# A fused attention, MoE and mixer kernel: the first third of the channel weights is combined before the token layer, and chunk 0's channel inputs are made before batch 1's first token product

## The chip, the cores and the metric

The kernel runs on one core of a Trainium2 chip. The metric is the time of one execution in microseconds (us), lower is better. The kernel before took 513.13 us (median of three runs, 512.84 to 515.15).

Engines are named as the profile names them: PE (TensorE, matmuls), PEld (its weight loads), DVE (VectorE), ACT (ScalarE), POOL (GpSimd) and SP (SyncE, which here only issues DMAs). Each runs its own list of instructions in order; semaphores tie the lists together.

## The reference

Three layers follow each other, on 2 batches of 768 tokens and 512 features.

```python
x = attention(q, k, v)                    # 8 heads, window and block sums
x = sigmoid(xr @ w_r) * (relu(xk @ w_k)**2 @ w_v)        # "MoE" layer
h = relu(x.T @ w_tok1) @ w_tok2           # token mixing, 768 -> 256 -> 768, per batch
u = x + h.T
out = u + relu(u @ w_ch1) @ w_ch2         # channel mixing, 512 -> 1536 -> 512
```

The weights arrive as 64-bit numbers and all products are made to about float32 precision.

## The kernel before

**Numbers in pairs.** Every operand of a product is split into a rounded part "hi" and a rest "lo", and `mm3` (L525 to L532) makes each product of three matmuls: hi by hi, hi by lo, lo by hi. ACT makes hi with a cast, DVE or POOL makes lo with a subtraction (`rounded`, L171 to L174; on L806 for the token layer's inputs `y`). So no product starts before its lo parts are there.

**Weights.** `Weights.step` takes one 128 x 512 piece of a weight matrix. SP has loaded it as 64-bit words into the slot (`wst`) that it will fill; ACT scales the upper words (L152), DVE puts the two halves together (a shift on L156 and a shift-or on L162), and then the pair is made on ACT and POOL. Pieces wait in one list and are taken in turn, one `step` at a time, at places that the code sets by credits.

**The channel layer's first product** is made by a Strassen scheme: seven products (`part(1)` to `part(7)`) of sums of quarter blocks take the place of eight. Its weights are therefore combined, not just split. `Fold.close` takes two pieces and makes of them, on DVE, POOL and ACT, the pairs that the seven products use: two sums by DVE or POOL of 128 x 512 elements, one of 128 x 256 by POOL, and four rounded pairs whose lo parts POOL makes. Two folds (d = 0 and 1) make one third (g = 0, 1, 2) of `w_ch1`. The unpacked pieces lie in a tile `f4` (`f` in the profile).

**The channel layer's inputs** are combined likewise, once per chunk of 512 tokens, by `chan_prep`. PE transposes four token tiles into `utr` (L841), ACT copies them into two tiles `f4`, and `first`, `second` and `third` make the pairs `u` for the seven products. All sums are DVE's (the default of `sums`, L184); of the lo parts, d = 0 is POOL's and d = 1 is DVE's:

```python
eng = nc.gpsimd, nc.vector
sums(pr[d], eng[d], (0, f[:, 1], f[:, 3], ALU.subtract), (1, f[:, 2], f[:, 0], ALU.subtract), tag=tags[d])
```

**The order of the work.** The attention and the MoE layer's first two products run interleaved; the loop over `gates` (the sigmoid product `ro`, L691 to L705) ends the MoE layer. Then `c_phase` runs, for batch 0 and batch 1: `y_split` (pairs of the token layer's input), `tok1` (36 matmuls into `h1`, in the profile `h`), `tok2` (36 into `ho`; L826 adds them to `ybuf`, the running result of all tokens). Before `d_phase`, the channel layer, stands `chan_prep(0)`:

```python
        yield from tok2(0, h0)
        h1 = yield from tok1(yy)
        uu = {}
        yield from chan_prep(0, uu)
        yield from tok2(1, h1)
```

Chunk 0 holds tokens 0 to 511 of batch 0, so it needs `tok2(0)` and nothing of batch 1. The code's order is a priority; a scheduler then sets each engine's order when the kernel is built, so that neighbouring steps overlap. `tc.high_priority(n)` moves steps ahead by n.

**Slots.** `wa` and `wb` (8 each) held the MoE layer's weights, `R2` (12, of which 10 are used) those of the gates and the token layer. When the MoE layer's tiles are free, pool `w2` is laid over them. In the kernel before, the second channel weights `w_ch2` (`c2_add`) go to `wb` and are first in the list of weights; `c1_add(0)` and `c1_add(1)` come behind them, into a ring `CR` of `w2`'s slots and freed ones.

Of the kernel before, what the change touches and what calls it, by code (L numbers as in the profile page):

```python
# [10 lines left out]
F32R = mybir.dt.float32r  # L11
# [38 lines left out]
AHEAD3 = 2  # L50
WF = 2
HC = 256
OB = 2


@with_exitstack
def fused_kernel(ctx, tc, q, k, v, vt, mu, w_k, w_v, w_r, w_t1, w_t2, w_c1, w_c2, out):
    nc = tc.nc
# [8 lines left out]
    KD = DM // 128  # L67
# [6 lines left out]
    CH = 512  # L74
# [5 lines left out]
    def bank(tag, bufs, shape, name):  # L80
        return ps.tile(shape, F32, tag=tag, bufs=bufs, name=name)

    const = pool("const", "left")
    ident = const.tile([128, 128], F32, name="ident")
# [8 lines left out]
    ys = [ybuf[:, i] for i in range(B * NT)]  # L93
# [18 lines left out]
    class Ring:  # L112
# [3 lines left out]
        def next(self):  # L116
            self.i += 1
            return self.slots[(self.i - 1) % len(self.slots)]
# [117 lines left out]
    weights = Weights()  # L236
# [4 lines left out]
    wa, wb = Ring(r1, "wa", NRA), Ring(r1, "wb", NRB)  # L241
# [436 lines left out]
    R2 = Ring(r2, "w", 12)  # L678
# [33 lines left out]
    for got in hidden:  # L712
# [4 lines left out]
        if len(wr) == KD:  # L717
            credit += (got or 0.0) * GRATIO
            while credit > 0:
                g = next(gates, None)  # L720
# [7 lines left out]
    U = Ring(r1, "u", 0)  # L728
    U.slots = wa.slots[:7]
    spare = wa.slots[7:]  # L730

    def c1_add(g):
        for d in range(2):
            fold = Fold(c1[g], CR, d, LEND[g][d])
            for z in (d, d + 2):
                weights.add(CR, w_c1[z * 128:(z + 1) * 128, :].rearrange("p (h f) -> p h f", h=2)[:, :, HC * g:HC * g + HC], fold)

    def tiles(g):
        return [2 * g, 2 * g + 1], [NF2 // 2 + 2 * g, NF2 // 2 + 2 * g + 1]

    def c2_add(c, g):
        for f in sum(tiles(g)[::-1], []):
            weights.add(wb, w_c2[f * 128:(f + 1) * 128, :], lambda pr, f=f: c2_have(f, pr))

    kept = ctx.enter_context(tc.tile_pool(name="kept", bufs=1, space=bass.MemoryType.DRAM))
    stored = {}
# [1 line left out]
    def c2_have(f, pr):  # L748
        c2[0, f] = pr
        t = stored[f] = kept.tile([128, 2, 512], F32, tag=f"w{f}", bufs=1, name="stored")  # L750
        for i in range(2):
            nc.sync.dma_start(t[:, i], pr[i].bitcast(F32))

    def c2_back(c, g):
        for f in sum(tiles(g)[::-1], []):
            t = wb.next().tile([128, 2, 512], F32R, "w")
            nc.gpsimd.dma_start(t, stored[f])  # L757
            c2[c, f] = t[:, 0], t[:, 1]

    c2_add(0, 0)  # L760
    credit = 0.0
    for got in gates:
        credit += got or 0.0
# [5 lines left out]
    xp.release()  # L769
    work.release()  # L770
    w2 = pool("w2", "left", reuse_waits="tile")
    CR = Ring(w2, "w", 21 - 12 - len(spare))
    CR.slots = spare + CR.slots + R2.slots[R2.i % 12:] + R2.slots[:R2.i % 12]
    LEND = CR.slots[12:14], CR.slots[14:15] * 2, (None, None)
    c1_add(0)
    c1_add(1)
    c2_add(0, 1)

    def new_f4():
        return w2.tile([128, 4, HC], F32, tag="f4", bufs=2, name="f4")  # L780
# [19 lines left out]
    def y_split(b):  # L800
        yy = []
        for s in range(NT):
            hi, lo = U.next().split("y")
            y = ys[b * NT + s]
            nc.scalar.copy(hi, y)
            (nc.vector if s % 2 else nc.gpsimd).tensor_tensor(lo, y, hi.bitcast(F32), ALU.subtract)  # L806
            yy.append((hi, lo))
        return yy

    def tok1(yy):  # L810
        hh = []
        for m in range(NM):
            o = bank("acc", MT, [128, DM], "h1")
            yield from mm3(o, [(cut(t1[s], m * 128, 128), yy[s]) for s in range(NT)])
            hh.append(relu_split(o))
        return hh

    def tok2(b, hh):
        for s0 in range(0, NT, 2):
            os = [bank(*(("s", 2) if s0 % 4 == 0 else ("acc", MT)), [128, DM], "ho") for _ in range(2)]  # L820
            for m in range(NM):
                for j in range(2):
                    yield from mm3(os[j], [(t2[s0 + j][m], hh[m])], first=(m == 0), last=(m == NM - 1))
            for j in range(2):
                y = ys[b * NT + s0 + j]
                nc.vector.tensor_tensor(y, os[j], y, ALU.add)  # L826
# [7 lines left out]
    def chan_prep(c, u):  # L834
        if c:
            fold_all()
        f4 = [new_f4() for _ in range(2)]
        for z in range(KD):
            tp = bank("pt", 2, [128, CH], "utr")
            for t in range(NQ):  # L840
                nc.tensor.transpose(tp[:, t * 128:(t + 1) * 128], ys[c * NQ + t][:, z * 128:(z + 1) * 128], ident)  # L841
            n = z // 2 * 2
            nc.scalar.copy(f4[z % 2][:, n:n + 2].rearrange("p a n -> p (a n)"), tp)
            yield 0.43
        eng = nc.gpsimd, nc.vector
        tags = (None,) * 6 if c else ("m3", "m4", "o", "o", "mw", "m4")

        @ahead(HM)
        def first():
            pr = [pieces(U.next(), "u") for _ in range(3)]  # L850
            for d in range(2):
                f = f4[d]
                sums(pr[d], eng[d], (0, f[:, 1], f[:, 3], ALU.subtract), (1, f[:, 2], f[:, 0], ALU.subtract), tag=tags[d])
                sums(piece(pr[2], d), eng[d], (0, f[:, 0], f[:, 3], ALU.add), tag=tags[2 + d])
                u[3, d], u[4, d], u[1, d] = piece(pr[d], 0), piece(pr[d], 1), piece(pr[2], d)

        @ahead(HM)
        def second():
            for d in range(2):
                pr = pieces(U.next(), "u")  # L860
                rounded(pr, f4[d][:, 0:4:3], eng[d])
                u[2, d], u[5, d] = piece(pr, 0), piece(pr, 1)

        @ahead(HM)
        def third():
            for d in range(2):
                pr = pieces(U.next(), "u")
                sums(pr, eng[d], (slice(0, 2), f4[d][:, 0::2], f4[d][:, 1::2], ALU.add), tag=tags[4 + d])
                u[6, d], u[7, d] = piece(pr, 0), piece(pr, 1)

        for make_some in first, second, third:
            make_some()
            yield 0.0

    def c_phase():
        yy = y_split(0)
        h0 = yield from tok1(yy)
        yy = y_split(1)
        yield from tok2(0, h0)
        h1 = yield from tok1(yy)  # L880
        uu = {}
        yield from chan_prep(0, uu)
        yield from tok2(1, h1)
        return uu

    def d_phase(uu):
# [39 lines left out]
        for n in range(nck * NG):  # L926
            c, g = divmod(n, NG)
            end = prev and prev[3] == NG - 1
            if g == 1 and c + 1 < nck:
                u2 = {}  # L930
                nxt = chan_prep(c + 1, u2)
            if n == 0:
                fold_all()
                c1_add(2)
            weights.early = c == 0
            o = yield from part(3, g, uu)
            s3 = copied("m3", o)
            o = yield from part(4, g, uu)
            s4 = copied("m4", o)
            w = w2.tile([128, 512], F32, tag="mw", bufs=1, name="mw")  # L940
            put(nc.vector, w, o, s3, ALU.add)
            o = yield from part(1, g, uu)
            put(nc.vector, w, o, w, ALU.add)
            if g == 2:
                next(nxt, None)
            if prev:
                yield from values2(prev[0], prev[2], prev[3], 0, 0, end)
            if g == 1:
                yield next(nxt, 0.0)
            o = yield from part(5, g, uu)  # L950
            put(nc.vector, o, o, s3, ALU.add)
            b12 = relu_split(o)
            put(nc.vector, s3, w, o, ALU.subtract)
            o = yield from part(2, g, uu)
            put(nc.vector, o, o, s4, ALU.add)
            b21 = relu_split(o)
            put(nc.vector, s4, w, o, ALU.subtract)
            if g == 2:
                next(nxt, None)
            if prev:  # L960
                yield from values2(prev[1], prev[2], prev[3], 1, 1, end)
                if n + 1 == 2:
                    c2_add(0, 2)
                elif n + 1 < nck * NG:
                    c2_back(*divmod(n + 1, NG))
            bring(1)
            if g == 1:
                yield next(nxt, 0.0)
            o = yield from part(7, g, uu)
            put(nc.vector, o, o, s3, ALU.add)  # L970
            b11 = relu_split(o)
            if g == 1:
                yield next(nxt, 0.0)
            o = yield from part(6, g, uu)
            put(nc.vector, o, o, s4, ALU.add)
            b22 = relu_split(o)
            if g == 2:
                next(nxt, None)
            bring(1)
            if g == 1:  # L980
                yield next(nxt, 0.0)
            yield from values2(b21, c, g, 1, 0)
            bring(1)
            yield from values2(b12, c, g, 0, 1)
            bring(1)
            prev = b11, b22, c, g
            if g == NG - 1:
                uu = u2 if c + 1 < nck else None
# [69 lines left out]
```

## Time and profile before

| what | value |
|---|---|
| median of 3 runs | 513.13 us (512.84 to 515.15) |
| the profiled execution's own time | 513.2 us |
| its span on the core | 511.4 us |
| PE busy | 489.1 us, 96% of the span |
| DVE busy | 326.4 us, 64% |
| POOL busy | 241.7 us, 47% |
| ACT busy | 233.9 us, 46% |
| mean granted clock of PE | 0.99 |

The profiled execution is 0.07 us above the median of the runs. The busy shares are means over the whole span, over stages that differ; the stages are told apart by views of single stretches. Times of instructions are from the start of the span. A duration in the profile holds an instruction's latency too, so that the next one on the engine can start up to 0.1 us before the first has ended (for a matmul 0.17 us); the distance of two starts is then the price of one in a row.

### The profile page before, as it was taken

Reading aid. Unit: us, or ns where it says so; the run is one execution under the profiler, and the core shown is the slowest. Engines: PE = TensorE matmul, PEld = TensorE weight load, DVE = VectorE, ACT = ScalarE, POOL = GpSimd, SP = SyncE. Lnnn points to the kernel's source line nnn. Section 1 sums busy time; section 2 is a strip of 40 time slices with the busy share of each in tenths; the row PEclk is TensorE's granted clock in tenths of the full one; section 3 lists DMA queues with packets and bytes.
Section 4 is the critical chain, followed back from the end, with each engine's and each line's share of the span. In section 5 each row is a group of like instructions: output and inputs, shape, how many; then the busy total and the mean of one; then the engine's idle time right before and its main releaser. Section 6 shows DMA issues by size and latency. Waiting matters only on the chain.

```text
span 511.4 us, 8956 instructions
## 1 busy us (share of the span) xinstructions
PE 489.1 (96%) x3388; PEld 410.3 (80%) x3388; DVE 326.4 (64%) x646; ACT 233.9 (46%) x531; POOL 241.7 (47%) x310
## 2 busy tenths in 40 slices
PE   7999897999999999999999978989999999999996
PEld 3578775888888888888887857978998998889885
DVE  3889999640605273898678689986965438354352
ACT  1789646862525454555457274456521234011110
POOL 5435577771534475697645885487610104001000
PEclk9999999999999999999999997999999999999999
DMA  8999922031001650003648320372826325173202
GB/s 264 313 310 364 331 67 76 7 96 42 19 1 22 235 198 0 1 0 87 214 153 282 96 76 0 124 248 82 248 60 187 114 53 164 34 215 92 74 0 83
DMA packets 32652, 64.36 MB, mean 126 GB/s; under 512 B 2880, under 2 KB 12096, under 8 KB 32608
## 3 DMA queue, kind: packets, MB, share of 16 engines
q1 hardware_dynamic: 29152, 51.20, 31.1%
q0 software_dynamic: 3456, 12.58, 8.8%
q8 instruction: 27, 0.44, 0.3%
q14 instruction: 17, 0.14, 0.1%
HBM read 53.74 MB, written 9.44 MB: 124 GB/s over the span
## 4 chain that ended last, share of the span: by engine, by line
PE 62%; DVE 17%; DMA 7%; POOL 4%; issue 4%; ACT 3%; SPq 2%; DVEq 0%; ACTq 0%; POOLq 0%
PE o L918 17%; PE m L530 15%; PE acc L530 11%; PE ko L530 10%; PE ro L530 4%; DMA ybuf<-in_v_dram 3%; DVE sum L184 2%; DMA wst<-in_moe_w_v_dram 2%; DVE xk L520 2%; DVE wf L162 2%; POOL w L174 2%; DVE wf L156 2%; PE h L530 1%; PE pv L419 1%; DVE f L162 1%
## 5 line engine op out<-in xcount | busy, mean ns | idle before, releaser
L530 PEld LDWEIGHTS m<-u,w 128*128 128x128 f32 x756 | 96.4, 193 | 7.0 <-ACT u L173 2.4
L530 PE MATMUL m<-u,w 128*128 128x256 f32 x756 | 98.6, 285 | 3.3 <-ACT u L173 2.1
L918 PE MATMUL o<-w,gh 128*128 128x512 f32 x288 | 89.4, 395 | 1.2 <-ACT gh L786 1.2
L530 PE MATMUL ko<-xh,w 128*128 128x256 f32 x384 | 76.6, 288 | 0.7 <-ACT w L173 0.6
L174 POOL TENSOR_TENSOR w<-wf,w 128x512 fp32r<-128x512 f32 x38 | 53.2, 1405 | 41.6 <-ACT w L173 39.5
L530 PEld LDWEIGHTS ko<-xh,w 128*128 128x128 f32 x384 | 61.2, 188 | 4.5 <-issue 1.4
L530 PE MATMUL acc<-w,kh 128*128 128x512 f32 x192 | 61.7, 404 | 1.9 <-ACT kh L544 1.9
L918 PEld LDWEIGHTS o<-w,gh 128*128 128x128 f32 x288 | 52.1, 188 | 11.9 <-ACT gh L786 1.4
L918 PE MATMUL o<-w,gl 128*128 128x512 f32 x144 | 55.9, 397 | 1.1 <-DVE gl L787 1.1
L530 PE MATMUL ko<-xl,w 128*128 128x256 f32 x192 | 54.5, 284 | 1.1 <-DVE xl L522 1.1
L545 POOL TENSOR_TENSOR kl<-rl,kh 128x512 fp32r<-128x512 f32 x24 | 34.5, 1439 | 34.5 <-ACT kh L544 31.1
L519 POOL TENSOR_SCALAR tmp<-xT,oms 128x256 f32<-128x256 f32 x52 | 38.1, 742 | 22.7 <-DVE xk L520 14.6
L786 ACT ACTIVATE gh<-m 128x512 fp32r<-128x512 f32 x36 | 21.4, 599 | 59.6 <-DVE m L798 59.5
L543 DVE TENSOR_TENSOR rl<-rl 128x512 f32<-128x512 f32 x24 | 18.5, 773 | 46.4 <-ACT rl L542 46.1
L382 ACT ACTIVATE pe<-pe,mn 128x120 f32<-128x120 f32 x96 | 36.6, 383 | 17.2 <-DVE mn L380 16.8
L757 POOL DMA_DIRECT2D w<-stored x24 | 13.1, 547 | 66.2 <-PE o L918 66.2
L530 PEld LDWEIGHTS acc<-w,kh 128*128 128x128 f32 x192 | 35.1, 191 | 9.4 <-ACT kh L544 2.4
L520 DVE SCALAR_TENSOR_TENSOR xk<-xT,mus,tmp 128x256 f32<-128x256 f32 x52 | 39.2, 784 | 4.3 <-POOL tmp L519 3.8
L798 DVE TENSOR_TENSOR m<-m,m 128x512 f32<-128x512 f32 x36 | 24.9, 695 | 26.7 <-PE m L530 26.2
L530 PE MATMUL acc<-w,kl 128*128 128x512 f32 x96 | 37.9, 406 | 1.1 <-POOL kl L545 1.1
L173 ACT CAST w<-wf 128x512 fp32r<-128x512 f32 x38 | 23.5, 619 | 31.5 <-DVE wf L162 31.4
L530 PEld LDWEIGHTS ko<-xl,w 128*128 128x128 f32 x192 | 36.2, 188 | 2.1 <-DVE xl L522 1.3
(104 smaller groups left out, 916.2 us busy)
## 6 DMA issues: line engine op xcount, KB each, us to landing
wst<-in_moe_w_ch_dram SPq DMA_DIRECT2D x24, 512.0 KB, 4.4
w<-stored POOLq DMA_DIRECT2D x24, 512.0 KB, 4.6
stored<-w SPq DMA_DIRECT2D x24, 256.0 KB, 4.9
wst<-in_moe_w_k_dram SPq DMA_DIRECT2D x8, 512.0 KB, 7.6
wst<-in_moe_w_v_dram SPq DMA_DIRECT2D x8, 512.0 KB, 9.4
kw<-in_k_dram SPq DMA_DIRECT2D x12, 320.0 KB, 8.6
wst<-in_moe_w_tok_dram SPq DMA_DIRECT2D x6, 512.0 KB, 4.6
out_dram<-o SPq DMA_DIRECT2D x12, 256.0 KB, 6.1
```

Of the source, the lines that this page charges most:

```text
L162: nc.vector.scalar_tensor_tensor(wi, top, 3, wi, ALU.logical_shift_left, ALU.bitwise_or)
L173: r = nc.scalar.copy(hi, src)
L174: eng.tensor_tensor(lo, src, hi.bitcast(F32), ALU.subtract)
L382: nc.scalar.activation(pe, pe, AF.Exp, bias=mn[:, p:p + 1], scale=-1.0, accum_out=den[:, p:p + 1])
L519: nc.gpsimd.tensor_scalar(tmp, xT[:, d, x0 - 1:x0 - 1 + MW], om[:, d:d + 1], 1.0, ALU.mult, ALU.mult)
L520: nc.vector.scalar_tensor_tensor(xk[:, d], xT[:, d, x0:x0 + MW], mu[:, d:d + 1], tmp, ALU.mult, ALU.add)
L530: nc.tensor.matmul(o, l, r, start=(first and i == 0), stop=(last and i == 3 * n - 1))
L543: nc.vector.tensor_tensor(rl, rl, rl, ALU.mult)
L545: nc.gpsimd.tensor_tensor(lo, rl, hi.bitcast(F32), ALU.subtract)
L786: nc.scalar.activation(hi, o, AF.Relu)
L798: eng.tensor_tensor(r, x, y, op)
L918: nc.tensor.matmul(accs[c][t], l, r, start=(first and j == 0 and i == 0), stop=(last and j == 1 and i == 2))
```

## The change

Five things change.

- `c1_add(0)` takes the place of `c2_add(0, 0)` as the first channel weights in the list, so that the first third of `w_ch1` is unpacked and folded while the gates run. It goes into `wb`, and its two `f4` tiles are the two slots of `R2` that nothing uses.
- `c2_add` gets a ring of its own of eight slots, `W2`, in pool `w2`. `c2_add(0, 0)` comes behind the first third, `c1_add(1)` behind it, and `c2_add(0, 1)` moves into `c_phase`, behind `tok1` of batch 1.
- `y_split(1)` gets slots of its own (four of `W2`, two of `U`), where it had one free slot and had to wait for batch 0's.
- `chan_prep(0)` is driven for six steps (its four transposes, `first` and `second`) between `tok2(0)` and `tok1` of batch 1; its transposes run at a priority of 100. `third` follows behind `tok1`.
- Both folds of the second third share one slot for `f4`.

The work itself is the same: no instruction of the arithmetic is added or dropped.

```diff
-    def c1_add(g):
+    def c1_add(g, ring, lend):
         for d in range(2):
-            fold = Fold(c1[g], CR, d, LEND[g][d])
+            fold = Fold(c1[g], ring, d, lend[d])
...
-    c2_add(0, 0)
+    c1_add(0, wb, R2.slots[10:])
     credit = 0.0
     for got in gates:
...
     w2 = pool("w2", "left", reuse_waits="tile")
-    CR = Ring(w2, "w", 21 - 12 - len(spare))
-    CR.slots = spare + CR.slots + R2.slots[R2.i % 12:] + R2.slots[:R2.i % 12]
-    LEND = CR.slots[12:14], CR.slots[14:15] * 2, (None, None)
-    c1_add(0)
-    c1_add(1)
-    c2_add(0, 1)
+    W2 = Ring(w2, "w", 8)
+    CR = Ring(w2, "w", 0)
+    CR.slots = wb.slots[7:] + spare + R2.slots[10:] + R2.slots[:10]
+    c2_add(0, 0)
+    c1_add(1, CR, CR.slots[7:8] * 2)
...
-            hi, lo = U.next().split("y")
+            hi, lo = (W2.slots[4:] + U.slots[5:] if b else U.slots)[s].split("y")
...
         for z in range(KD):
-            tp = bank("pt", 2, [128, CH], "utr")
...
+            with tc.high_priority(HU) if not c else ExitStack():
+                tp = bank("pt", 2, [128, CH], "utr")
...
         yy = y_split(1)
         yield from tok2(0, h0)
+        uu = {}
+        prep = chan_prep(0, uu)
+        for _ in range(KD + 2):
+            yield next(prep)
         h1 = yield from tok1(yy)
-        uu = {}
-        yield from chan_prep(0, uu)
+        c2_add(0, 1)
+        yield from prep
         yield from tok2(1, h1)
```

`HU` is 100; `c2_add` and `c2_back` use `W2` where they used `wb`; `c1_add(2)` goes to `CR` as before.

**DVE, from the token layer's first `h1` of batch 1 on.** The names: `gl` is the lo part of a token or channel product, `sum` a sum of quarter blocks (of weights where it reads `f4_3361`, of chunk 0's inputs where it reads `f4_3483` and `f4_3484`), `u` the lo part of such an input, and the add into `ybuf` frees a bank of `tok2`. In the kernel before:

```order
L787 SCALAR_TENSOR_TENSOR gl_3435<-h1_3409,gh_3434 128x512
L162 SCALAR_TENSOR_TENSOR f4_3361<-wst_3318,f4_3361 128x512
L162 SCALAR_TENSOR_TENSOR f4_3361<-wst_3359,f4_3361 128x512
L787 SCALAR_TENSOR_TENSOR gl_3480<-h1_3438,gh_3479 128x512
L184 TENSOR_TENSOR sum_3395<-f4_3361 128x512
L826 TENSOR_TENSOR ybuf_71<-ho_3558,ybuf_71 128x512
L184 TENSOR_TENSOR sum_3524<-f4_3483 128x256
L184 TENSOR_TENSOR sum_3549<-f4_3483 128x512
L184 TENSOR_TENSOR sum_3524<-f4_3483 128x256
L184 TENSOR_TENSOR sum_3529<-f4_3483 128x256
L826 TENSOR_TENSOR ybuf_71<-ho_3559,ybuf_71 128x512
```

And in the changed kernel, where the same tiles have other numbers (chunk 0's are `f4_3409` and `f4_3410`):

```order
L787 SCALAR_TENSOR_TENSOR gl_3508<-h1_3462,gh_3507 128x512
L163 SCALAR_TENSOR_TENSOR f4_3361<-wst_3328,f4_3361 128x512
L163 SCALAR_TENSOR_TENSOR f4_3361<-wst_3359,f4_3361 128x512
L185 TENSOR_TENSOR sum_3438<-f4_3409 128x256 x2
L185 TENSOR_TENSOR sum_3443<-f4_3409 128x256
L185 TENSOR_TENSOR sum_3535<-f4_3409 128x512
L185 TENSOR_TENSOR sum_3395<-f4_3361 128x512
L185 TENSOR_TENSOR sum_3447<-f4_3410 128x256 x2
L185 TENSOR_TENSOR sum_3452<-f4_3410 128x256
L175 TENSOR_TENSOR u_3459<-f4_3410,u_3459 128x512
L787 SCALAR_TENSOR_TENSOR gl_3531<-h1_3511,gh_3530 128x512
L826 TENSOR_TENSOR ybuf_71<-ho_3544,ybuf_71 128x512
```

Eight sums and the lo part `u_3459` have moved ahead of the second `gl` of batch 1 and of the first add of `tok2` into `ybuf`.

**POOL, in the same stretch of the changed kernel,** where `w` is the lo part of a weight pair:

```order
L175 TENSOR_TENSOR w_3286<-wf_3282,w_3286 128x512
L175 TENSOR_TENSOR w_3334<-wf_3330,w_3334 128x512
L185 TENSOR_TENSOR sum_3399<-f4_3361 128x512
L175 TENSOR_TENSOR u_3456<-f4_3409,u_3456 128x512
L175 TENSOR_TENSOR w_3389<-f4_3361,w_3389 128x512
L175 TENSOR_TENSOR u_3435<-sum_3438,u_3435 128x512
L175 TENSOR_TENSOR u_3437<-sum_3443,u_3437 128x256
L175 TENSOR_TENSOR w_3391<-sum_3399,w_3391 128x512
L175 TENSOR_TENSOR u_3534<-sum_3535,u_3534 128x512
L175 TENSOR_TENSOR w_3390<-sum_3395,w_3390 128x512
L185 TENSOR_TENSOR sum_3403<-f4_3361 128x256
```

Nine of its instructions, from `sum_3399` to `sum_3403`, now read what the same two DVE instructions on `f4_3361` and the copies of chunk 0 release; the lo parts of two `w_ch2` pieces (`w_3286`, `w_3334`) stand ahead of them, where the second fold of the first third stood.

**PE, behind `tok1` of batch 1 in the changed kernel** (`ho` is `tok2`, `m` a Strassen product):

```order
L531 MATMUL ho_3574<-gh_3507,w_2819 128x512
L531 MATMUL m_3688<-u_3456,w_3117 128x256 x3
L531 MATMUL m_3688<-u_3459,w_3177 128x256
L531 MATMUL m_3618<-u_3435,w_3116 128x256
L531 MATMUL m_3645<-u_3435,w_3116 128x256
L531 MATMUL ho_3544<-gh_3530,w_2765 128x512
L531 MATMUL ho_3545<-gh_3530,w_2765 128x512
L531 MATMUL ho_3574<-gh_3530,w_2819 128x512
L531 MATMUL m_3688<-u_3459,w_3177 128x256 x2
```

In the kernel before, the matmuls on the same input (there `u_3545`) come behind all of `tok2(1)`; here its first one comes behind 9 of `tok2`'s 36 matmuls, and the two in the last row, of which the first takes the lo part of `u_3459`, behind 12.

## Rows read from the trace of the kernel before

**Rows 1.** The page, part 1: busy us, share of the span, instructions of each engine.

```profile
PE 489.1 (96%) x3388; PEld 410.3 (80%) x3388; DVE 326.4 (64%) x646; ACT 233.9 (46%) x531; POOL 241.7 (47%) x310
```

**Rows 2.** Busy time by stretch (us, PE, PEld, DVE, ACT, POOL, clock, DMA).

```profile
301.90:309.90 8.00, 3.84 (x14) 2.68 (x12) 8.00 (x10) 3.55 (x7) 7.38 (x7) 0.79 0.20 66
309.90:317.80 7.90, 7.86 (x54) 7.86 (x55) 7.63 (x13) 3.05 (x6) 3.16 (x2) 0.78 0.00 0
317.80:345.60 27.80, 25.45 (x159) 21.96 (x157) 26.09 (x36) 15.24 (x28) 18.46 (x15) 1.00 0.50 171
```

**Rows 3.** Timeline of PE, 275 to 346: start, us, operation, [idle before it <- releaser].

```profile
275.46 0.50 PE L530 MATMUL ho<-gl,w 128*128 128x512 f32 x1 [1.25 <-DVE gl L787]
...
284.35 8.48 PE L530 MATMUL h<-y,w 128*128 128x512 f32 x36
292.67 0.60 PE L841 MATMUL utr<-ident,ybuf 128*128 128x128 f32 x4
293.03 0.71 PE L530 MATMUL ho<-gh,w 128*128 128x512 f32 x2
...
295.99 0.97 PE L530 MATMUL ho<-gh,w 128*128 128x512 f32 x3 [0.62 <-ACT gh L786]
...
304.26 0.50 PE L530 MATMUL m<-u,w 128*128 128x256 f32 x2 [2.13 <-ACT u L173]
305.63 0.50 PE L530 MATMUL ho<-gh,w 128*128 128x512 f32 x1 [0.86 <-DVE ybuf L826]
...
309.94 7.99 PE L530 MATMUL m<-u,w 128*128 128x256 f32 x53 [1.22 <-DVE u L174]
317.77 1.09 PE L918 MATMUL o<-w,gh 128*128 128x512 f32 x4
319.18 0.73 PE L918 MATMUL o<-w,gl 128*128 128x512 f32 x2 [0.32 <-DVE gl L787]
...
321.15 2.96 PE L530 MATMUL m<-u,w 128*128 128x256 f32 x24
323.95 1.09 PE L918 MATMUL o<-w,gh 128*128 128x512 f32 x4
...
342.64 2.13 PE L918 MATMUL o<-w,gh 128*128 128x512 f32 x8 [1.23 <-ACT gh L786]
345.57 0.74 PE L918 MATMUL o<-w,gl 128*128 128x512 f32 x2 [0.81 <-DVE gl L787]
```

**Rows 4.** Timeline of DVE, 294 to 345.

```profile
294.93 1.38 DVE L162 SCALAR_TENSOR_TENSOR f<-wst,f 128x512 int32<-128x512 int32 x2 [2.37 <-ACT wst L152]
...
300.03 4.94 DVE L184 TENSOR_TENSOR sum<-f 128x256 f32<-128x256 f32 x4 [1.01 <-ACT f L843]
...
305.50 3.20 DVE L184 TENSOR_TENSOR sum<-f 128x256 f32<-128x256 f32 x3
...
314.42 0.68 DVE L184 TENSOR_TENSOR sum<-f 128x512 f32<-128x512 f32 x1
315.37 0.70 DVE L798 TENSOR_TENSOR m<-m,m 128x512 f32<-128x512 f32 x1 [0.27 <-ACT m L793]
...
316.74 1.78 DVE L174 TENSOR_TENSOR u<-sum,u 128x512 fp32r<-128x512 f32 x1
...
344.84 0.68 DVE L787 SCALAR_TENSOR_TENSOR gl<-m,gh 128x512 fp32r<-128x512 f32 x1
```

**Rows 5.** Timeline of POOL, 299 to 309.

```profile
299.42 2.73 POOL L174 TENSOR_TENSOR w<-sum,w 128x512 fp32r<-128x512 f32 x2
302.10 1.18 POOL L184 TENSOR_TENSOR sum<-f 128x256 f32<-128x256 f32 x1
303.24 1.45 POOL L174 TENSOR_TENSOR u<-f,u 128x512 fp32r<-128x512 f32 x1
304.65 3.76 POOL L174 TENSOR_TENSOR u<-sum,u 128x512 fp32r<-128x512 f32 x3
```

**Rows 6.** Timeline of ACT, the copies of chunk 0's last transposes.

```profile
299.42 1.07 ACT L843 COPY f<-utr 128x512 f32<-128x512 f32 x2
```

More of the change, by code (lines that the diff above doesn't have):

```diff
@@ L52 @@
 HC = 256
+HU = 100
 OB = 2
@@ L730, in fused_kernel @@
     spare = wa.slots[7:]
-    def c1_add(g):
+    def c1_add(g, ring, lend):
         for d in range(2):
-            fold = Fold(c1[g], CR, d, LEND[g][d])
+            fold = Fold(c1[g], ring, d, lend[d])
             for z in (d, d + 2):
-                weights.add(CR, w_c1[z * 128:(z + 1) * 128, :].rearrange("p (h f) -> p h f", h=2)[:, :, HC * g:HC * g + HC], fold)
+                weights.add(ring, w_c1[z * 128:(z + 1) * 128, :].rearrange("p (h f) -> p h f", h=2)[:, :, HC * g:HC * g + HC], fold)
     def tiles(g):
@@ L742, in c2_add @@
         for f in sum(tiles(g)[::-1], []):
-            weights.add(wb, w_c2[f * 128:(f + 1) * 128, :], lambda pr, f=f: c2_have(f, pr))
+            weights.add(W2, w_c2[f * 128:(f + 1) * 128, :], lambda pr, f=f: c2_have(f, pr))
     kept = ctx.enter_context(tc.tile_pool(name="kept", bufs=1, space=bass.MemoryType.DRAM))
@@ L755, in c2_back @@
         for f in sum(tiles(g)[::-1], []):
-            t = wb.next().tile([128, 2, 512], F32R, "w")
+            t = W2.next().tile([128, 2, 512], F32R, "w")
             nc.gpsimd.dma_start(t, stored[f])
             c2[c, f] = t[:, 0], t[:, 1]
-    c2_add(0, 0)
+    c1_add(0, wb, R2.slots[10:])
     credit = 0.0
@@ L838, in chan_prep @@
         for z in range(KD):
-            tp = bank("pt", 2, [128, CH], "utr")
[L840 to L843, printed above, removed]
+            with tc.high_priority(HU) if not c else ExitStack():
+                tp = bank("pt", 2, [128, CH], "utr")
+                for t in range(NQ):
+                    nc.tensor.transpose(tp[:, t * 128:(t + 1) * 128], ys[c * NQ + t][:, z * 128:(z + 1) * 128], ident)
+                n = z // 2 * 2
+                nc.scalar.copy(f4[z % 2][:, n:n + 2].rearrange("p a n -> p (a n)"), tp)
             yield 0.43
@@ L933, in d_phase @@
                 fold_all()
-                c1_add(2)
+                c1_add(2, CR, (None, None))
             weights.early = c == 0
```

## Prediction

> **What bounds the kernel now.** First the page's busy shares: TensorE is busy for 489.1 us, 96% of the span [rows 1], and the change adds no matmul. All it can win is TensorE time that is idle or slow, so the next view is the timeline of TensorE with what ended each wait. From the token layer's second half to the middle of the first channel group there are eight waits: 1.25 us at 275, then 0.62, 2.13, 0.86 and 1.22 us between 296 and 310, then 0.32, 1.23 and 0.81 us up to 346, 8.44 us in all [rows 3]. The table of stretches adds the clock: 0.79 of full speed in the 8 us from 301.9 and 0.78 in the 7.9 us after them [rows 2]. [...]
>
> Third, the waits are VectorE's doing. It is busy in all 8.00 us from 301.9 and in 26.09 of the 27.8 us from 317.8 [rows 2]. In its own timeline [rows 4] the seven sums of chunk 0 take 4.94 and 3.20 us between 300.03 and 308.7; one 128 x 512 sum alone, at 314.42, takes 0.68. GpSimd's timeline [rows 5] shows why: it works without a gap over the same time, and seven VectorE sums end in the time of seven GpSimd instructions. They take turns. Seven in 308.7 - 300.03 = 8.7 us is 1.24 us for each.
>
> **The first third, folded earlier.** Eight unpack instructions of `w_c2` leave VectorE's list during the gates and eight of the first third take their place, with two sums more. On VectorE that is nearly even, since the old list had two long instructions of the next weights there. GpSimd gets two folds, each four 512-wide instructions (2.73 / 2 = 1.37 us) and two 256-wide (1.18): 2 x 7.8 = 15.7 us [rows 5]. They start when the second piece is unpacked, around 263, and end around 279, or 283 with the three lo parts of `y` put between them. `tok1` of batch 1 starts at 284.35 [rows 3], so the cover holds by a little. The wait of 1.25 us at 275 is for a `gl` behind a weight instruction; now a sum stands there instead, and the `gl` after it stands behind two `y`: 1.25 stays, within -0.8 and +1.0. I take +0.3, so `tok1` starts at 284.65. The copies into ring `W2` instead of `wb` change no count; its first loads must wait for the gates' last reads but are wanted ten microseconds later: nothing.
>
> **Chunk 0, made earlier.** [...] On TensorE's new list the second matmul on `u_3459` stands behind 12 of `tok2`'s 36 matmuls, not behind all, and 24 of `tok2` with 54 Strassen matmuls are queued behind it. So I work out when TensorE arrives there and when VectorE delivers.
>
> TensorE: 36 matmuls of `tok1` at (292.67 - 284.35) / 36 = 0.231 us, 8.3; ten transposes at (293.03 - 292.67) / 4 = 0.09, 0.9; 12 of `tok2` at 0.231, 2.8; six Strassen matmuls at (323.95 - 321.15) / 24 = 0.117, 0.7 [rows 3]. It arrives at 284.65 + 12.7 = 297.4.
>
> VectorE: the sums of chunk 0 need the third block of transposes, behind 30 matmuls of `tok1` and six transposes (284.65 + 6.9 + 0.5 = 292.1), and an ACT copy of 0.53 [rows 6]: 292.6 at the earliest. ACT has weights to cast in front of it whose release runs over GpSimd, 2 us more if these are late; I take 293.5. From there eight sums and the lo part `u_3459` stand in a row, and beside them nine GpSimd instructions that nothing else holds up. At 1.24 us they take 11.1; but three of the nine are 512 wide where one of seven was, so 12.0. The bounds: 3.9 us if GpSimd were out of the way (three at 0.6, six 256-wide at about half of the 0.68 of the row at 314.42), and 12.6 if each pair also takes the longer half of the turns seen. `u_3459` is there at 305.5, with ends 296.5 and 307.2.
>
> The new wait is then 305.5 - 297.4 = 8.1 us in one piece, where there were 4.83 in four. Behind it lie 54 x 0.117 + 24 x 0.231 = 11.9 us of matmuls up to the first `o`. The clock will fall again, for the gap is longer than the one that TensorE had before the fall [rows 2]; what of it lies behind the gap costs between 0 and 3.4 us (half of 6.8), and I take half, 1.7. The first `o` comes at 305.5 + 11.9 + 1.7 = 319.1, where it came at 317.77: 1.3 us later.
>
> [...]
>
> **After the first `o`.** The waits left there, 0.32, 1.23 and 0.81, are VectorE's list running late: it works almost without a pause from its first `m` (315.37) to the `gl` at 344.84 [rows 4]. In the new order its first `m` waits for the 24 matmuls of `tok2`: 305.5 + 5.5 + 24 x 0.117 + 1.7 = 315.5, with an add and an unpack behind it 316.8, so 1.4 later; but a lo part of 1.78 us (at 316.74) now lies ahead of it. So VectorE's `gl` comes 0.4 us earlier, and TensorE, without waits, would be there at 319.1 + 25.4 = 344.5. Between this -0.4 and the +1.3 I take +0.6. Behind 346 I take the two orders as equal.
>
> The sum: 513.2 + 0.6 = **513.8 us**, no change that a measurement of this kernel can tell (0.5%, 2.6 us, to either side).
>
> **The rivals.** *Faster: the sums pass GpSimd.* If GpSimd stalls between its nine (its lo parts wait for ACT's casts of VectorE's sums), VectorE runs at 0.68 or less and `u_3459` comes near 297.4. TensorE then waits for nothing until the first `o` at 309.3. VectorE's list bounds the rest: it loses its pauses of 2.37, 1.01 and 0.27 us before its first `m` and the 1.78, 5.4 in all: 507.8. For it: ACT's list is long there. Against: the weights' lo parts keep GpSimd supplied, and seven sums in a row show no stall before.
>
> [...]
>
> *The gates get longer.* The folds delay `tok2(0)` by 2 to 3 us: 516. It needs GpSimd's `y` after 287; against it stands the order, with the `y` between the folds. That the change does not do what it says is excluded by the order: the folds and the transposes have moved.
>
> **How the numbers follow.** My forecast of no change gets 0.52, faster 0.21, the long wait with the slow clock 0.22, the longer gates 0.05. The range reaches nearly to the faster rival, at 509.0, and to the slower one with a little over, 517.6; what is left out is the better half of the faster case and the tail of the slower. Faster by over 0.5% (below 510.6) is the first rival, 0.21; slower by over 0.5% (above 515.7) is the other two, 0.27; within, 0.52.
>
> **What would show it.** In the profile after: no wait of 2.13 us for ACT's `u`; one wait of 6 to 9 us for DVE's `u` that ends near 305; a clock near 0.8 over the 10 us behind it; nine VectorE instructions at over 1.2 us each beside an unbroken GpSimd; the first `o` between 318 and 321. [...]

## The result and the profile after

The changed kernel takes 517.0 us (median of 9 runs, 515.55 to 517.62) where the kernel before took 513.13 (9 runs): a ratio of 1.0066, 95% interval 1.0051 to 1.0082. It is slower, by more than the 0.5% that a measurement of this kernel can tell. Here and below, ratios and intervals leave out single executions over 1.5% above the fastest of the same kernel, medians do not. The profiled execution took 517.5 us, its span is 515.7.

The page, part 1, of the changed kernel; TensorE's busy time is that of [rows 1] within 0.3 us:

```profile
PE 489.4 (95%) x3388; PEld 411.4 (80%) x3388; DVE 331.4 (64%) x646; ACT 232.2 (45%) x531; POOL 242.4 (47%) x310
```

Timeline of TensorE, changed kernel (start, us, operation, [idle before it <- releaser]), for [rows 3]:

```profile
257.22 4.02 PE L531 MATMUL h<-y,w 128*128 128x512 f32 x17
...
280.90 0.50 PE L531 MATMUL ho<-gl,w 128*128 128x512 f32 x1 [0.85 <-DVE gl L787]
...
287.17 2.11 PE L531 MATMUL h<-y,w 128*128 128x512 f32 x8
...
300.01 0.38 PE L531 MATMUL m<-u,w 128*128 128x256 f32 x1 [0.75 <-ACT u L174]
302.84 1.43 PE L531 MATMUL m<-u,w 128*128 128x256 f32 x5 [2.44 <-POOL u L175]
304.07 1.48 PE L531 MATMUL ho<-gh,w 128*128 128x512 f32 x3
311.84 2.29 PE L531 MATMUL m<-u,w 128*128 128x256 f32 x9 [6.29 <-DVE u L175]
...
325.42 1.09 PE L923 MATMUL o<-w,gh 128*128 128x512 f32 x4
...
349.07 2.11 PE L923 MATMUL o<-w,gh 128*128 128x512 f32 x8 [0.36 <-ACT gh L786]
```

The wait of 2.13 us for ACT's `u` is gone, and a wait of 6.29 us for VectorE's `u` is there. With the 0.75 and the 2.44 ahead of it, 9.5 us of TensorE are idle before the first `o`, where [rows 3] have 4.83. Behind the first `o` the three waits of before, 2.36 us, have shrunk to 0.36.

Busy time by stretch, changed kernel (us, PE, PEld, DVE, ACT, POOL, clock, DMA), for [rows 2]:

```profile
13.00:26.00 13.00, 12.15 (x95) 6.53 (x90) 9.93 (x41) 8.93 (x37) 5.07 (x14) 0.87 1.09 288
...
300.60:314.30 13.70, 5.17 (x18) 4.32 (x19) 11.79 (x9) 5.68 (x11) 11.77 (x9) 0.53 0.55 217
314.30:325.40 11.10, 11.10 (x69) 9.94 (x68) 10.38 (x17) 3.74 (x8) 2.71 (x3) 0.96 0.16 47
325.40:350.00 24.60, 24.23 (x154) 21.68 (x153) 24.22 (x34) 14.06 (x25) 16.91 (x13) 1.00 0.53 178
```

In the traces of both kernels the granted clock is 1.00 or 0.50 of full speed and nothing between. At 0.50 a Strassen matmul takes 0.232 us (nine from 311.84 to 313.93 in the changed kernel), at 1.00 it takes 0.119 (nine from 317.27 to 318.34). So the clock is at half speed for (0.47 x 13.7 + 0.04 x 11.1) / 0.5 = 13.8 us, twice the (0.21 x 8.0 + 0.22 x 7.9) / 0.5 = 6.8 of before [rows 2]. But 7.7 of them fall into the two long waits (the whole 6.29, and 1.4 of the 2.44, in which the mean clock is 0.72), so about 6 us of work ran at half speed and 3.0 us were lost, nearly as in the kernel before, where the wait of 1.22 us lies in the 6.8 and the other 5.6 lost 2.8. Of the 3.0, 1.6 lie behind the 6.29 us wait, for the clock is back at full speed at 315.1.

The first line is a surprise: the clock also fell between 13 and 26 us, in the attention, where both kernels run the same lists. That costs 0.13 x 13 = 1.7 us, and the edit changes no instruction there. To take it out, times below are counted from the start of `tok1` of batch 0 (257.22 here). A second profile of the kernel before (`before_again`, below) happens to have the same early fall, and is what the changed kernel is best compared with:

```profile
13.00:26.00 13.00, 12.15 (x96) 6.54 (x88) 10.02 (x41) 8.99 (x37) 5.04 (x13) 0.87 1.09 296
```

```profile
257.15 4.05 PE L530 MATMUL h<-y,w 128*128 128x512 f32 x17
...
286.15 8.48 PE L530 MATMUL h<-y,w 128*128 128x512 f32 x36
...
319.55 1.09 PE L918 MATMUL o<-w,gh 128*128 128x512 f32 x4
```

From `tok1` of batch 0 it is 29.00 us to `tok1` of batch 1 (changed kernel 29.95), 62.40 to the first `o` (68.20) and 256.0 to the end of the span (513.2 - 257.15; changed kernel 258.5). So the change loses 5.8 us up to the first `o`, gets 3.3 back behind it, and costs 2.5 us. The other 1.4 of the 3.9 between the medians are not traced to a cause. The start of the kernel is the likeliest part of them, since the rest repeats (first two runs below).

### The profile page after: what moved, and what is told of

Same layout as the page of the kernel before. It is cut to its first block, busy times and chain, and to the rows that moved or that the text cites. A ratio compares the mean times of both kernels' runs of the same rounds, so it can differ in the third digit from the quotient of the medians.

```text
span 515.7 us, 8958 instructions
## 1 busy us (share of the span) xinstructions
PE 489.4 (95%) x3388; PEld 411.4 (80%) x3388; DVE 331.4 (64%) x646; ACT 232.2 (45%) x531; POOL 242.4 (47%) x310
## 4 chain that ended last, share of the span: by engine, by line
PE 61%; DVE 18%; DMA 7%; POOL 5%; issue 4%; ACT 2%; SPq 2%; DVEq 0%; POOLq 0%; ACTq 0%
PE o L923 16%; PE m L531 14%; PE acc L531 11%; PE ko L531 10%; PE ro L531 4%; DMA ybuf<-in_v_dram 3%; DVE sum L185 3%; DVE xk L521 2%; DVE wf L157 2%; DMA wst<-in_moe_w_v_dram 2%; POOL w L175 2%; DVE wf L163 2%; DMA wst<-in_moe_w_k_dram 2%; PE h L531 1%; PE pv L420 1%
## 5 line engine op out<-in xcount | busy, mean ns | idle before, releaser
L923 PE MATMUL o<-w,gh 128*128 128x512 f32 x288 | 88.3, 391 | 0.4 <-ACT gh L786 0.4
L520 POOL TENSOR_SCALAR tmp<-xT,oms 128x256 f32<-128x256 f32 x52 | 38.1, 742 | 22.7 <-DVE xk L521 14.6
L531 PE MATMUL acc<-w,kl 128*128 128x512 f32 x96 | 37.9, 406 | 1.1 <-POOL kl L546 1.1
## 6 DMA issues: line engine op xcount, KB each, us to landing
stored<-w SPq DMA_DIRECT2D x24, 256.0 KB, 3.6
out_dram<-o SPq DMA_DIRECT2D x12, 256.0 KB, 6.2
```

The source lines that it names most:

```text
L520: nc.gpsimd.tensor_scalar(tmp, xT[:, d, x0 - 1:x0 - 1 + MW], om[:, d:d + 1], 1.0, ALU.mult, ALU.mult)
L531: nc.tensor.matmul(o, l, r, start=(first and i == 0), stop=(last and i == 3 * n - 1))
L923: nc.tensor.matmul(accs[c][t], l, r, start=(first and j == 0 and i == 0), stop=(last and j == 1 and i == 2))
```

## The experiments

Eleven runs, each timed in rounds beside the kernel before on the same chip. The last two columns count from the start of `tok1` of batch 0 in the profiled execution; the end is that of the span, 3.8 to 3.9 us behind the last matmul, to which two of the expectations count.

| run | median us | ratio to before, 95% interval | first `o` | end of span |
|---|---|---|---|---|
| before_again | 513.34 | 1.0000 [0.9985, 1.0015] | 62.4 | 256.0 |
| after_again | 517.13 | 1.0057 [1.0038, 1.0076] | 69.1 | 259.3 |
| prep_late | 514.79 | 1.0041 [1.0009, 1.0072] | 65.3 | 257.6 |
| c1_1_late | 516.83 | 1.0052 [1.0022, 1.0083] | 60.1 | 258.0 |
| gl_first | 515.65 | 1.0036 [1.0014, 1.0058] | 63.6 | 259.6 |
| gl_first_c1late | 513.26 | 0.9994 [0.9975, 1.0014] | 57.9 | 255.4 |
| copies_first | 513.79 | 0.9985 [0.9958, 1.0011] | 60.5 | 256.3 |
| copies_gl | 515.43 | 1.0040 [1.0024, 1.0055] | 60.1 | 258.2 |
| copies_slower | 516.16 | 1.0049 [1.0031, 1.0067] | 60.5 | 257.3 |
| copies_add_first | 510.20 | 0.9935 [0.9914, 0.9956] | 60.5 | 253.0 |
| copies_add_first3 | 511.46 | 0.9956 [0.9940, 0.9973] | 60.5 | 253.7 |

**How much is the start.** Both kernels once more, unedited.

> The changed kernel itself once more, nothing edited. Theory (1.7 of its 4.3 us of span belong to the first 255 us, where both kernels run the same lists, and come from TensorE's clock at the start, which differs from execution to execution): in this profile the stretch from the start of tok1 of batch 0 to the end is again about 258.5 us long, the new waits (0.75, 2.44 and 6.3 us) are there again, while tok1 of batch 0 may start anywhere from 254.7 to 260; the median over several rounds is 515 to 517. Rival (the change itself delays the early part): tok1 of batch 0 starts at 257 or later again and the fastest run is above 517.

> The kernel before once more, nothing edited, for a second profile. Theory: from the start of tok1 of batch 0 to the last matmul it is 252 us again (252.2 before, 254.6 and 255.4 in two profiles of the changed kernel), so that 2.4 to 3.2 us are the change's own; tok1 of batch 0 starts between 254.5 and 261. Its o matmuls take 0.233 us each in a row again (0.227 in the changed kernel). Rival: that stretch differs by over 1 us between two profiles of one kernel, and the 2.4 us say little.

In the changed kernel's second profile the waits are 0.75, 2.46 and 6.67 us. `tok1` of batch 0 starts at 261.5 this time, because the clock was at 0.67 from 13 to 26 us and 0.82 from there to 40; this execution took 522.7 us, and the comparisons go by the first profile. The kernel before repeats its eight waits to 0.02 us. The stretch behind `tok1` of batch 0 repeats to 0.1 us in the kernel before and to 0.8 in the changed one. Its start does not: it lies at 255.4 and 257.15 in the two profiles of before, at 257.2 and 261.5 in those of the changed kernel, at 254.7 to 260.0 in the other nine. Whether the changed kernel's executions fall there more often was not tried, and why the clock falls in some and not in others was not found.

**Only the first third early.** `chan_prep(0)` goes back behind `tok1` of batch 1, and `HU` is 0.

```diff
-        prep = chan_prep(0, uu)
-        for _ in range(KD + 2):
-            yield next(prep)
         h1 = yield from tok1(yy)
         c2_add(0, 1)
-        yield from prep
+        yield from chan_prep(0, uu)
```

> Keeps the first third's early folds and the new slots, but makes chunk 0's inputs behind tok1 of batch 1 again, as the kernel before did. Theory (the loss is the new wait for the lo part of chunk 0's second input and the slow clock with it): the one wait of 6.3 us goes, waits of 0.5 to 2.2 us between 296 and 311 come back, 4 to 5 us in all, the clock is at half speed for about 7 us instead of 13.7, the first o comes near 319 and the time is 513 to 514.5 us. Rival (the folds lengthen the gates): tok1 of batch 1 still starts about 2.8 us later than before, and the time stays at 516 to 517.

```profile
308.37 0.69 PE L531 MATMUL m<-u,w 128*128 128x256 f32 x2 [1.97 <-ACT u L174]
...
314.04 8.69 PE L531 MATMUL m<-u,w 128*128 128x256 f32 x53 [0.53 <-DVE u L175]
```

TensorE's timeline has the four waits of before again, 4.7 us in all, and none of 6. The first `o` is 2.9 us earlier than in the changed kernel, later than expected, and the end 0.9. So the moved inputs make the long wait. But by the end they are only 0.9 of the 2.5 us, and the run is still 0.4% slower than before: what else was changed (the first third's folds, the slots, the order of the weights, which this run does not part) costs something too. At `tok1` of batch 1 it is 0.7 us (29.72). Then the clock is at half speed for 10.2 us, where about 7 were expected and the kernel before has 6.8 (the clock is the third figure from the end):

```profile
308.40:318.80 10.40, 9.20 (x34) 8.04 (x35) 10.40 (x17) 2.32 (x5) 5.05 (x6) 0.51 0.01 4
```

The other 3.4 us at half speed cost 1.7. Whether the fall is as long in other executions of this run was not tried.

**Nothing folded beside the sums.** The second third's weights join the list behind `tok1` of batch 1.

```diff
-    c1_add(1, CR, CR.slots[7:8] * 2)
...
         h1 = yield from tok1(yy)
+        c1_add(1, CR, CR.slots[7:8] * 2)
         c2_add(0, 1)
```

> Adds the second third's weights to the list behind tok1 of batch 1, so that no weight is folded while VectorE makes chunk 0's sums. Theory (VectorE and GpSimd take turns, and that sets the sums' rate): seven sums and the lo part take 4 to 5 us in place of 12.0 for nine, the lo part is there at 300 to 303, the wait for it is under 2 us, the first o comes at 316 to 319 and the time is 507 to 513 us, the upper end if the second third's folds are then late for the second channel group. Rival (the place in VectorE's queue, whatever GpSimd does): the sums are still spaced by over 1.1 us, the wait stays over 5 us and the time at 516 to 517.

Timeline of VectorE, of GpSimd and of TensorE in this run:

```profile
293.75 6.89 DVE L185 TENSOR_TENSOR sum<-f 128x256 f32<-128x256 f32 x7 [0.91 <-ACT f L843]
300.56 0.68 DVE L175 TENSOR_TENSOR u<-f,u 128x512 fp32r<-128x512 f32 x1
```

```profile
294.80 1.58 POOL L175 TENSOR_TENSOR u<-f,u 128x512 fp32r<-128x512 f32 x1 [0.54 <-ACT u L174]
296.33 4.03 POOL L175 TENSOR_TENSOR u<-sum,u 128x512 fp32r<-128x512 f32 x3
```

```profile
301.29 2.77 PE L531 MATMUL m<-u,w 128*128 128x256 f32 x14 [3.28 <-DVE u L175]
...
342.37 3.27 PE L923 MATMUL o<-w,gh 128*128 128x512 f32 x8 [4.47 <-ACT gh L785]
```

GpSimd has four instructions beside the sums instead of nine, and is done at 300.36. The lo part, which starts just then, takes 0.68 us; in the changed kernel the same instruction took 1.75. From the first sum to the end of the lo part it is 7.5 us for eight instructions, not 12.0 for nine (4 to 5 were expected). But the edit does not change GpSimd alone: without the weights in front of the copies, the sums also start 39.0 us behind `tok1` of batch 0 and not 42.6. The wait falls from 6.29 to 3.28 (more than expected was left) and the first `o` comes 8.1 us earlier. Nearly all of it is lost again behind the first `o`, most in one new wait of 4.47 us for `gh`: the rival's time, though not for the rival's reason.

**The queue on VectorE.** The sums of quarter blocks are held behind the second `gl` (`behind` fixes the order of two instructions in one engine's list and adds no wait; `los` lists the `gl` instructions, `hold` those that a sum must follow). Only the six sums of 128 x 256 are held, not seven as the expectations have it: the one of 128 x 512 belongs to `third`, which runs when `hold` is empty again, and it passes `gl`. The second run adds the edit above.

```diff
-        for _ in range(KD + 2):
+        for _ in range(KD):
             yield next(prep)
         h1 = yield from tok1(yy)
+        hold.append(los[-1])
+        for _ in range(2):
+            yield next(prep)
+        hold.clear()
...
-            adder.tensor_tensor(s[:, a], x, y, op)
+            r = adder.tensor_tensor(s[:, a], x, y, op)
+            if adder is nc.vector:
+                behind(r, hold)
```

> Holds chunk 0's seven sums of quarter blocks on VectorE behind the second gl of batch 1's tok1; the sums come as early in the code as tok1 allows. Theory (the queue: the matmuls of tok2 wait because gl stands behind the sums, and the lo part too): gl ends near 302 and the lo part before it, no wait for the lo part over 3 us, the first o at 319 to 321 in place of 325.4, the time 511.5 to 514. Rival (only the sums' own rate counts, TensorE ends up waiting for the last of them): the same 6 us stand somewhat later, in front of the first matmul on a sum's pair, and the time is 515.5 to 517.

> Both edits together: the sums behind the second gl, and the second third's weights added behind tok1 of batch 1. Theory (turns and queue both): all waits between 296 and 318 are under 2 us in all, the clock stays at full speed there or falls for under 4 us, the first o comes at 314 to 317 and the time is 505 to 511 us. Rival (the second third's folds come late in place of it): a wait of 3 to 6 us in front of the second channel group near 345, and the time is 511 to 516.

VectorE and TensorE in `gl_first`:

```profile
300.25 1.70 DVE L175 TENSOR_TENSOR u<-f,u 128x512 fp32r<-128x512 f32 x1
301.87 0.68 DVE L789 SCALAR_TENSOR_TENSOR gl<-h,gh 128x512 fp32r<-128x512 f32 x1
302.47 7.47 DVE L185 TENSOR_TENSOR sum<-f 128x256 f32<-128x256 f32 x6
```

```profile
344.76 3.78 PE L929 MATMUL o<-w,gh 128*128 128x512 f32 x8 [2.73 <-ACT gh L788]
```

The lo part and `gl` pass the sums, the long wait splits into 1.86, 1.85 and 1.51, and the first `o` comes 4.6 us earlier, as expected; six sums beside GpSimd still take 7.47 us. The time misses the expectation, for a wait of 2.73 us for `gh` opens later, with a slow clock behind it (0.52 from 344.76 to 351.00). With both edits one wait of 1.17 us is left before the first `o`, which comes 10.3 us earlier though 12 more matmuls stand ahead of it. Here GpSimd waits for a cast while four of the six sums run, and the six take half as long:

```profile
302.48 3.70 DVE L185 TENSOR_TENSOR sum<-f 128x256 f32<-128x256 f32 x6
```

```profile
343.22 2.11 PE L929 MATMUL o<-w,gh 128*128 128x512 f32 x8 [3.59 <-ACT gh L787]
```

But 7.8 us of waits appear later, of which this 3.59 is the largest, and the run ends level with the kernel before.

**The copies on ScalarE.** The scaling of the last `w_ch2` piece and of the next two pieces is held behind the copy of chunk 0's last transpose (`acts` lists the scalings).

```diff
             after(a)
             behind(a, self.rounded[-2:-1])
+            acts.append(a)
...
-                nc.scalar.copy(f4[z % 2][:, n:n + 2].rearrange("p a n -> p (a n)"), tp)
+                r = nc.scalar.copy(f4[z % 2][:, n:n + 2].rearrange("p a n -> p (a n)"), tp)
+                if not c and z == 3:
+                    for a in acts[-3:]:
+                        behind(a, [r])
```

> On ScalarE, the scaling of the last w_ch2 piece and of the second third's first two pieces is held behind the copy of chunk 0's last transpose. Theory (the lo part came late because the copies stood behind weight casts; GpSimd's turns then did the rest): the copies follow the transposes at once, the third 38.5 us behind the start of tok1 of batch 0 (41.2 in the changed kernel), the lo part of the second input ends at 46 to 49 behind it (54.6), the wait for it is 0 to 3 us, the first o comes at 61 to 64 (68.2), and the time is 511.5 to 514. Rival (the sums' rate beside GpSimd alone sets it): the lo part still ends later than 51 and the time stays over 515.

> The same hold on ScalarE, and the seven sums of quarter blocks held behind the second gl of batch 1. Theory: gl ends before 45 us behind the start of tok1 of batch 0, no wait over 2 us stands before the first o, which comes at 59 to 62, and the time is 509 to 513. Rival (what is won before the first o is given back behind it, because VectorE's list is as long as before): the first o comes that early, but waits of 3 us or more for gh and gl stand between 80 and 100 us behind tok1 of batch 0, and the time is 512.5 to 515.

ScalarE, VectorE and TensorE in `copies_first`:

```profile
294.23 1.07 ACT L845 COPY f<-utr 128x512 f32<-128x512 f32 x2 [0.73 <-PE utr L843]
```

```profile
295.55 6.49 DVE L186 TENSOR_TENSOR sum<-f 128x256 f32<-128x256 f32 x7
...
302.56 0.68 DVE L176 TENSOR_TENSOR u<-f,u 128x512 fp32r<-128x512 f32 x1
...
338.88 3.44 DVE L164 SCALAR_TENSOR_TENSOR f<-wst,f 128x512 int32<-128x512 int32 x2
342.25 0.69 DVE L799 TENSOR_TENSOR m<-m,m 128x512 f32<-128x512 f32 x1
```

```profile
303.30 2.50 PE L532 MATMUL m<-u,w 128*128 128x256 f32 x14 [3.65 <-DVE u L176]
...
343.62 3.78 PE L927 MATMUL o<-w,gh 128*128 128x512 f32 x8 [3.65 <-ACT gh L787]
```

The copies now wait for TensorE alone and start 37.9 us behind `tok1` of batch 0 (41.2 in the changed kernel). The lo part ends at 46.9 (54.6), the first `o` comes 7.7 us earlier, and the median is level with before. The lo part gains 7.7 us: 3.4 because the sums start at 39.2 and not 42.6, and 4.3 because the fold behind the held pieces starts later: GpSimd has four instructions beside the sums and not nine, and VectorE has seven sums and an unpack instruction before the lo part and not eight sums. So this one hold on ScalarE, which brings the copies forward and puts the next fold back, takes the change's loss away; how much each of the two would do without the other was not tried. Up to the first `o` it does what `c1_1_late` does; behind it, it loses 2.1 us less. `copies_gl` is 1.6 us slower: its first `o` is at 60.1, and behind it stand 4.77 and 1.66 us of waits, as its rival says.

**The wait that opens later.** The last rows of VectorE and TensorE above show what it is: VectorE's add of a product stands behind two unpack instructions of 3.44 us. The first try slows the list of weights in the channel layer (5 units of credit for a step, not 3). The second and third hold the last two, or three, unpack instructions behind that add:

```diff
-            put(nc.vector, o, o, s3, ALU.add)
+            p = put(nc.vector, o, o, s3, ALU.add)
+            if n == 1:
+                for x in uns[-2:]:
+                    behind(x, [p])
             b12 = relu_split(o)
```

(`uns` lists the unpack instructions; `put` now returns its own.)

> The hold of the weight casts behind chunk 0's copies, and in the channel layer a step of the weights for every 5 units of credit in place of 3, so that VectorE unpacks the last third's pieces later. Theory (the wait of 3.65 us for gh at 87 us behind tok1 of batch 0 is VectorE's add standing behind two unpack instructions of 3.44 us): that wait is under 2 us, no other one over 1.5 us takes its place, and the time is 509.5 to 512, less than both kernels. Rival (the weights are then late for the third channel group): a wait of 2 us or more for w or gh stands between 100 and 120 us behind tok1 of batch 0, and the time is 512 to 515.

> The hold of the weight casts behind chunk 0's copies, and VectorE's add of the second group's fifth product held ahead of the two last unpack instructions of the third third's second fold. Theory (the 3.65 us wait for gh is that add standing behind them): the add comes 2.2 us earlier, as soon as the product is there, the wait falls to 1 to 2 us, from the start of tok1 of batch 0 to the end it is 249.5 to 251 us (252.4 with the first hold alone, 252.2 in the kernel before), and the time is 510 to 512.5, the lowest of all. Rival (VectorE's list is full there, so that the next add or gl is late in its place): the waits between 80 and 110 us behind tok1 of batch 0 still sum to over 3 us and the time is 512.5 to 514.

> The same with the third unpack instruction and its sum held behind that add too. Theory: VectorE then idles before the add, the add comes no earlier than in the other run, and the third third's folds come 1 to 2 us later: the time is within 1 us of the other run. Rival: the later fold makes a wait of over 1.5 us for a weight between 95 and 110 us behind tok1 of batch 0, and the time is 1.5 us or more above the other run.

Slower weights cut the wait to 1.36 us and open one of 2.94 for a weight, 101 us behind `tok1` of batch 0: the rival, and at 516.16 us slower than the rival said. Holding the two behind the add works. VectorE and TensorE in `copies_add_first`:

```profile
337.82 0.69 DVE L799 TENSOR_TENSOR m<-m,m 128x512 f32<-128x512 f32 x1
338.42 2.86 DVE L164 SCALAR_TENSOR_TENSOR f<-wst,f 128x512 int32<-128x512 int32 x2
```

```profile
340.24 2.12 PE L927 MATMUL o<-w,gh 128*128 128x512 f32 x8 [1.34 <-ACT gh L787]
```

The add comes 3.4 us earlier (82.5 behind `tok1` of batch 0, not 85.9), the wait is 1.34, and the kernel takes 510.20 us, 0.65% less than the kernel before beside it; it is the only version, with its sibling, that beats both kernels. The end gains 3.3 us on `copies_first`, and the waits are the smaller part of it: behind the first `o` they sum to 2.5 us (1.34 and a new one of 1.19), where they were 3.65. The larger part is the clock. In `copies_first` it falls at that wait, so that eight `o` matmuls take 3.78 us and not 2.12; here it stays at 1.00 from 338.90 to 348.00. In `copies_first` (the clock is the third figure from the end):

```profile
341.80:348.80 7.00, 5.18 (x12) 4.12 (x13) 5.50 (x9) 4.29 (x8) 5.57 (x5) 0.51 0.22 87
```

Holding three is 1.3 us slower by the medians and 0.7 by the profiles, between the two expectations.

## Why the prediction was right and wrong

The range (509.0 to 517.6) holds the result, 0.6 us below its upper end. The forecast of no change (513.8) missed it by 3.2 us. Point by point:

**The mechanism was right.** A long wait for `u_3459`, behind VectorE's eight sums, stands in the place of four shorter ones; the clock is at 0.50 around it, from 301.5 to 315.1; the gates are nearly even. Two shorter waits ahead of it, 0.75 and 2.44 us for other inputs made from the same copies, were not foreseen. The price of the nine was right as well: VectorE and GpSimd of the changed kernel,

```profile
299.82 10.29 DVE L185 TENSOR_TENSOR sum<-f 128x256 f32<-128x256 f32 x8
310.04 1.75 DVE L175 TENSOR_TENSOR u<-f,u 128x512 fp32r<-128x512 f32 x1
311.71 0.68 DVE L787 SCALAR_TENSOR_TENSOR gl<-h,gh 128x512 fp32r<-128x512 f32 x1
```

```profile
300.05 1.32 POOL L185 TENSOR_TENSOR sum<-f 128x512 f32<-128x512 f32 x1 [1.30 <-DVE f L163]
301.33 1.45 POOL L175 TENSOR_TENSOR u<-f,u 128x512 fp32r<-128x512 f32 x1
...
311.20 1.17 POOL L185 TENSOR_TENSOR sum<-f 128x256 f32<-128x256 f32 x1
```

from 299.82 to 311.79, 12.0 us; 12.0 was the term. GpSimd works without a gap from 300.05 on. The turns are not even, so that the exact hit is partly luck: the first sum took 0.33 us, before GpSimd began, and the others 0.9 to 1.7. The lo part of 512 elements took 0.68 us where the runs show GpSimd at rest (`u` in `c1_1_late` and `copies_first`), and 1.75 here, beside it.

**The term that failed: "I take 293.5", the start of the nine behind the copies.** It was put 38.1 us behind `tok1` of batch 0 (293.5 less the 255.4 of that profile). They started at 42.6. ScalarE and VectorE of the changed kernel show why:

```profile
296.75 0.62 ACT L174 CAST w<-wf 128x512 fp32r<-128x512 f32 x1 [1.97 <-DVE wf L163]
297.28 1.21 ACT L153 ACTIVATE wst<-wst 128x512 f32<-128x512 f32 x2
298.39 1.06 ACT L844 COPY f<-utr 128x512 f32<-128x512 f32 x2
```

```profile
294.41 1.52 DVE L157 TENSOR_SCALAR wf<-wst 128x512 int32<-128x512 int32 x1 [1.20 <-POOL w L175]
296.03 0.69 DVE L163 SCALAR_TENSOR_TENSOR wf<-wst,wf 128x512 int32<-128x512 int32 x1
...
297.97 1.93 DVE L163 SCALAR_TENSOR_TENSOR f<-wst,f 128x512 int32<-128x512 int32 x2 [0.65 <-ACT wst L153]
```

The transposes were done at 295.5 and the copies started at 298.4. In front of them stood a cast that waited for VectorE's unpack, which waited for GpSimd to free its buffer, and two scalings of 1.2 us; and then VectorE's own next two unpacks stood in front of the sums. The prediction had seen this chain ("2 us more if these are late") and taken a small part of it. `copies_first` shows the term's worth: with that queue gone the sums start at 39.2, so that it is 3.4 of the 4.5 us. The gates, +0.95 where "+0.3" was taken, are in the rest.

**The terms that follow.** `u_3459` came 54.6 us behind `tok1` of batch 0, not 50.1, and the first `o` is 5.8 us late instead of 1.3. The 4.5 us are the whole miss there, for the rest of that sum held: from the first matmul behind the wait to the first `o` it is 13.6 us (11.9 + 1.7), of which the clock lost 1.6. The 1.7 was the author's choice between 0 and 3.4, and no run shows it as a term; measured are 3.3 us at a clock of 0.50 behind the long wait, up to 315.1, which lost the 1.6. One term was off by more and cost nothing: TensorE reached that matmul 48.3 us behind `tok1` of batch 0, not 42.0, mostly for the 3.2 us of the two waits ahead and 1.4 us lost to the slow clock between them and the long one. So the long wait is 6.29 us and not 8.1, but what set the first `o` was the lo part, which came later still. The gap before the fall of the clock is not what [rows 2] gives, though no term hangs on it: the fall comes at 306.5, inside the 8 us in which TensorE is busy for 3.84, and ahead of it lie the waits of 2.13 and 0.86 us [rows 3].

**The second term that failed: "+0.6" behind the first `o`.** It gave back 0.7 of the 1.3; measured are 3.3 of 5.8. VectorE's list bounds that stretch (24.22 us busy of the 24.60 from 325.40), and a TensorE that comes later finds it done: 2.0 us of late waits vanish. The experiments are the other side of it: the edits that bring the first `o` forward by 8 us meet a new wait of 3 to 5 us there, as long as VectorE's list is left as it is. The remaining 1.3 are matmul time. The `o` matmuls gain more than that: the distances from one to the next sum to 2.2 us less than before, of which the Strassen matmuls give back 1.2. Three `o` matmuls in a row take 0.69 to 0.70 us in the kernel before and 0.68 in the changed one (first `before_again`, then the changed kernel):

```profile
506.43 0.63 PE L918 MATMUL o<-w,gh 128*128 128x512 f32 x2
...
507.12 0.63 PE L918 MATMUL o<-w,gh 128*128 128x512 f32 x2
```

```profile
505.51 0.62 PE L923 MATMUL o<-w,gh 128*128 128x512 f32 x2
...
506.19 0.62 PE L923 MATMUL o<-w,gh 128*128 128x512 f32 x2
```

**The slower rival,** the long wait with the slow clock (0.22), is near the result partly by chance. The wait came, and the lo part was later than forecast (310.0 in that profile's time, not 305.5) by the casts ahead of the copies; but behind the wait the clock was slow for only 3.3 us, up to 315.1. Like for like the mechanism costs 2.5 us, which makes 515.7 of the profiled 513.2; the rest of 517.0 is not accounted for, and the likeliest part of it is the start of the kernel, which no step of the prediction speaks of. **The faster rival** needed GpSimd to stall between its nine; it did not.

## What to carry to other kernels

When work is moved earlier, price the queue that its inputs stand in, on every engine of the chain, as carefully as the work: here the price of the sums held to a tenth of a microsecond and their start was 4.5 us off. A move that brings one engine's work forward pays only where the next bound lets it through; two edits of the order, one on ScalarE and one on VectorE, took the change from 517.0 to 510.2 us with no work removed, while what the other edits won before the first `o` was mostly given back behind it. A wait costs more than its length when the clock falls with it: behind the 3.65 us of `copies_first` eight `o` matmuls took 3.78 us at a clock of 0.51, behind the 1.34 of `copies_add_first` 2.12 at 1.00. Compare kernels from a point where their lists part, and profile each twice: the start alone moved by up to 6.8 us between executions.

## What was not expected of the hardware

- Within the first 40 us, where both kernels have the same lists, the clock granted to TensorE fell in some executions and not in others: 1.00 and 0.87 from 13 to 26 us in two profiles of the kernel before, 0.87 and 0.67 in two of the changed one. At worst, with 0.82 in the next 14 us, this cost 0.33 x 13 + 0.18 x 14 = 6.8 us.
- One VectorE lo part of 128 x 512 took 1.75 us beside a busy GpSimd and 0.68 with GpSimd idle, in the same place of the program. So a fold on GpSimd costs VectorE time too: here 1.07 us on this one instruction.
- The `o` matmul takes 0.227 us in a row in the changed kernel and 0.233 in the one before. Their operands lie in other slots (`W2` for `wb`); that this is the cause was not tried.
